# A hash-attention kernel with a feed-forward layer: another order for the first batch

## The chip, the cores and the metric

The kernel runs on one core of a Trainium2 chip. The metric is the device time of one execution in microseconds; lower is better. Profiles come from one profiled execution each, whose own time stands beside its span.

## What is computed

Four batches of eight heads attend over 768 positions with 64 values per head. Each query and key gets a bucket from six sign bits, and a query sees only the keys of its own bucket. The heads' outputs, side by side, are the input of a feed-forward layer that takes the largest of three products.

```python
q_bits = (np.einsum('bhsd,dk->bhsk', q, proj) > 0)      # 6 bits, k likewise
mask   = q_bucket[:, :, :, None] == k_bucket[:, :, None, :]
scores = np.where(mask, scale * q @ k.T, -1e9)
attn   = softmax(scores)                                 # + 1e-09 in the denominator
x      = (attn @ v) as [3072, 512]
h      = np.maximum(np.maximum(x @ w1, x @ w2), x @ w3)  # [3072, 768]
out    = h @ w_out                                       # [3072, 512]
```

## The kernel before

The mask is part of the matmul: six (or eight) rows of plus or minus one half stand below the 64 rows of queries and keys in the S tiles, so that a score of unequal buckets comes out far lower, and the exp takes it to almost nothing.

The work is cut into units. A unit is one head, half of the queries (384) and two of the six key blocks: `scores(u)` issues two matmuls into one of two PSUM buffers, and ScalarE takes the exp of both into a ring of 18 AT tiles. Six units make a group, which is one pair of heads and one half of the queries (`qh`); 32 groups make 192 units, 48 for each batch. The list `groups` sets their order.

When a group's six exps are done, `values(g)` (24 small matmuls) makes the attention output, and sums of the exps (24 small matmuls with ones) make the denominators. `far` does two groups with one set of sums: `part_values` twice, `part_sums`, `invert` (VectorE transposes and reciprocal, then five GpSimd copies that spread the result), and `scale` for each group, which writes `xT`. `near` does one group by itself without the GpSimd copies. The PSUM tile of the values has one buffer.

The feed-forward for half a batch (`ffn_groups(h)`) is 24 pieces: 18 of the first layer (four matmuls and a VectorE maximum each) and 6 halves of the second layer. It needs `xT` of all four pairs of that half. The list `ffn` hands out one piece per step.

The order is written out by hand and each engine runs its own instructions in that order (manual_schedule). Step u of the main loop issues `scores(u + 1)`, then what `when(u, ...)` put down for the step, then due steps such as `scale`, then one feed-forward piece if there is one, then what `firsts[u]` holds (values, sums), and from the second batch on a `burst` every twelve units.

Preparation of the first batch goes by pairs of heads. `pair_group` transposes three blocks on TensorE into PSUM and copies them to a T32 tile on VectorE; `pair_place` writes them as bfloat16 into S on GpSimd; `pair_hash` multiplies by the projection, VectorE makes the bits, and SyncE's queue sends them into S in four DMAs. Pair 0 has a way of its own (`first_hash`, `first_place`, `first_bits`), with its first unit started early. Later heads go by quads: `load_quad` and `load_v` load them, `turn` transposes on VectorE, `narrow` converts on GpSimd, `place` and `quad_hash` send into S by DMAs on SyncE's queue. `load_weights` loads w1, w2, w3 and w_out on GpSimd's queue.

Before, the first batch's groups are both halves of pair 0, both halves of pair 1, the first half of pairs 2 and 3, then their second half. So the first half of the queries is complete with the sixth group, and its feed-forward starts with step 40.

Of the kernel before, what the change touches and what calls it, by code (L numbers as in the profile page):

```python
# [9 lines left out]
FP32 = mybir.dt.float32  # L10
# [7 lines left out]
def kernel(  # L18
# [15 lines left out]
    P = 128  # L34
# [79 lines left out]
    def pair_keep(pi, side, hd, mp):  # L114
        if pi not in t32:
            t32[pi] = t32_pool.tile([P, 2, S], FP32, tag="T32", name="T32")
        nc.vector.tensor_copy(t32[pi][:, side, hd * HALF : (hd + 1) * HALF], mp[:, 0:HALF])  # L117

    def pair_place(pi, side, par, h0=0, h1=2):
        o = s_tile(pi)[0:D, 2 * side + h0 : 2 * side + h1, par * HALF : (par + 1) * HALF]  # L120
        i_ = t32[pi][par * D : (par + 1) * D, side, h0 * HALF : h1 * HALF].rearrange("d (h n) -> d h n", n=HALF)
        nc.gpsimd.tensor_scalar(out=o, in0=i_, scalar1=RS, scalar2=1.0, op0=AluOp.mult, op1=AluOp.mult)  # L122
# [27 lines left out]
    def first_hash(bp, side, hd):  # L150
        for par in range(2):
            j = 2 * side + par
            nc.tensor.matmul(bp[Q * j : Q * j + NBITS, 0:HALF], pj2[:, par : 2 * NBITS : 2],  # L153
                             t32[0][:, side, hd * HALF : (hd + 1) * HALF], start=True, stop=True)

    def first_bits(bp, side, hd, par):
        j = 2 * side + par
        nc.vector.tensor_scalar(out=s_of[0][D : D + NBITS, 2 * side + hd, par * HALF : (par + 1) * HALF],  # L158
                                in0=bp[Q * j : Q * j + NBITS, 0:HALF], scalar1=0.0, scalar2=0.5,
                                op0=AluOp.is_gt, op1=AluOp.subtract)  # L160
# [64 lines left out]


    groups = [(b, qh, jj) for b in range(B) for qh in range(2) for jj in range(HPAIR)]
    groups[0:8] = [(0, g % 2, g // 2) for g in range(4)] + [(0, g // 2, 2 + g % 2) for g in range(4)]
    NU = len(groups) * UPG
    UPB = NU // B  # L230
    xts, avs_of, av_of, sm_of = {}, {}, {}, {}
# [1 line left out]

    def unit_of(u):
        g, n = divmod(u, UPG)
        if g < 4:
            hd, n = divmod(u % (2 * UPG), UPG)
            return 2 * (g // 2) + n // MH, hd, n % MH
        return g, n // MH, n % MH

    def place_of(g, hd, kp):
        if g < 4:
            return (g // 2) * 2 * UPG + hd * UPG + (g % 2) * MH + kp
        return g * UPG + hd * MH + kp

    def scores(u):
        g, hd, kp = unit_of(u)
# [40 lines left out]
    def inverse(o, sm):  # L288
        ys = ys_pool.tile([P, HALF], FP32, tag="ys", name="ys")
        rr = small.tile([P, HALF // Q], FP32, tag="rr", name="rr")  # L290
        nc.vector.transpose(ys[:], sm[:, 0:HALF])
        nc.vector.tensor_scalar(out=rr[:], in0=ys[:, 0:HALF:Q], scalar1=EPS * S, scalar2=None, op0=AluOp.add)
        nc.vector.reciprocal(rr[:], rr[:])
        nc.vector.transpose(o, rr[:].unsqueeze(2).to_broadcast((P, HALF // Q, Q)))  # L294
# [25 lines left out]
    def far(gs):  # L320
        avs, sms, sb = [], [], []

        def part_values(i):
            if not sb:
                sb.append(small.tile([P, 2], FP32, tag="sv", name="sv"))
                sb.append(rb_pool.tile([P, 2, HALF], FP32, tag="rb", name="rb"))
            sv = sb[0]
            av = values(gs[i])
            avs.append(avs_pool.tile([P, HALF + 4], FP32, tag="avs", name="avs"))
            nc.vector.tensor_copy(avs[i][:, 0 : HALF + 1], av[:, 0 : HALF + 1])  # L330
            nc.gpsimd.tensor_scalar_mul(sv[:, i : i + 1], avs[i][:, HALF : HALF + 1], EPS)  # L331

        def part_sums():
            sms.append(ms_ps.tile([P, 512], FP32, tag="ms", name="sm"))
            for m in range(NM):
                for r in range(4):
                    nc.tensor.matmul(sms[0][Q * r : Q * (r + 1), 0:HALF], ones[:, :],  # L337
                                     at_of(gs[r % 2], m, r // 2)[:, 0:HALF], start=(m == 0), stop=(m == NM - 1))

        def invert():  # L340
            rb = sb[1]
            inverse(rb[:, 0, :], sms[0])
            nc.gpsimd.tensor_copy(rb[:, 1, :], rb[:, 0, :])  # L343
            for p0 in (0, D):
                nc.gpsimd.tensor_copy(rb[p0 + Q : p0 + D, 0, :], rb[p0 : p0 + Q, 0, :])  # L345
            for p0 in (0, D):
                nc.gpsimd.tensor_copy(rb[p0 : p0 + Q, 1, :], rb[p0 + Q : p0 + D, 1, :])  # L347

        def scale(i):
            sv, rb = sb  # L350
            nc.vector.scalar_tensor_tensor(out=xt_of(gs[i]), in0=avs[i][:, 0:HALF], scalar=sv[:, i : i + 1],  # L351
                                           in1=rb[:, i, :], op0=AluOp.add, op1=AluOp.mult)

        return part_values, part_sums, invert, [(6 + i, lambda i=i: scale(i)) for i in range(2)]


    def ffn_groups(h):
# [34 lines left out]
    def when(u, f, *args):  # L392
        at.setdefault(u, []).append(lambda: f(*args))

    with tc.manual_schedule():
# [39 lines left out]
            first_place(side, 0, par, mp)  # L435
            first_bits(bp, side, 0, par)
        pair_place(0, 0, 1, 0, 1)
        first_bits(bq, 0, 0, 1)
        mq1 = ms_ps.tile([P, 512], FP32, tag="ms", name="mp")
        pair_turn(0, 0, 1, mq1)  # L440
        scores(0)
        pair_keep(0, 1, 1, mk1)
        pair_keep(0, 0, 1, mq1)

        def first_rest():
            bps = [ms_ps.tile([P, 512], FP32, tag="ms", name="bp") for side in range(2)]
            for side in (1, 0):
                first_hash(bps[side], side, 1)
                for par in range(2):
                    pair_place(0, side, par, 1, 2)  # L450
            for side, par in ((1, 0), (0, 0), (1, 1), (0, 1)):
                first_bits(bps[side], side, 1, par)
            t32.pop(0)

        when(0, first_rest)

        for pi, us, uh in ((1, (1, 2, 3, 4), 6), (2, (8, 9, 14, 15), 16), (3, (17, 18, 19, 20), 21)):
            for u, (side, hd) in zip(us, ((1, 0), (1, 1), (0, 0), (0, 1))):
                when(u, pair_group, pi, side, hd)
                if hd == 1:  # L460
                    for par in range(2):
                        when(u, pair_place, pi, side, par)
            when(uh, pair_hash, pi)
        when(14, load_v, 1)
        for n, u in enumerate((1, 9, 22, 30)):
            when(u, load_weights, n)
        for u, side, g in ((8, 0, 2), (23, 1, 3), (25, 0, 3)):
            when(u, load_quad, side, g, range(4), nc.sync)
        hash_at = {}
        for g in range(2, NPAIR // 2):  # L470
            b2, i2 = divmod(g, 2)
            need = UPB * b2 + 12 * i2
            for n, side in enumerate((1, 0)):
                name = (side, g)
                if g > 3:
                    for x in range(4):
                        when(need - 36 + 4 * n + x, load_quad, side, g, (x,), nc.gpsimd)
                t0 = need - (24 if g == 2 else 21) + 4 * n
                for n2 in range(4):
                    when(t0 + n2, turn, name, n2 // 2, n2 % 2)  # L480
                for u2 in range(2):
                    when(t0 + 2 + 2 * u2, narrow, name, u2)
                when(t0 + 6, place, name, range(4))
            hash_at[{2: 34, 3: 50}.get(g, need - 12)] = g
            when({2: 33, 3: 44}.get(g, need - 22), load_v, g)

        ffn, steps = [], []
        ffn_at = {40: 0, 57: 1, **{24 * (h + 1) + 9: h for h in range(2, 2 * B - 1)}}

        def hash_due(u):  # L490
            if u in hash_at:
                when(u + 1, quad_hash(hash_at[u]))

        def burst(u, gs):
            vals, sums, invert, late = far(gs)
            vals(0)
            sums()
            hash_due(u)
            vals(1)
            invert()  # L500
            steps.extend((u + n, f) for n, f in late)


        firsts = {}

        def far_at(gs, us):
            vals, sums, invert, late = far(gs)
            for i, u in enumerate(us):
                firsts[u] = [lambda i=i: vals(i)]
            firsts[us[1] + 1] = [sums, invert, lambda: steps.extend((us[1] + 1 + n, f) for n, f in late)]  # L510

        def near_at(g, u):
            vals, sums = near(g)
            firsts[u], firsts[u + 1] = [vals], [sums]

        far_at((0, 1), (10, 12))
        far_at((2, 3), (22, 24))
        near_at(4, 30)
        near_at(5, 36)
        far_at((6, 7), (42, 48))  # L520
        for u in (34, 50):
            firsts[u] = [lambda u=u: hash_due(u)]

        for u in range(NU):
            if u + 1 < NU:
# [60 lines left out]
```

## Time and profile before

| | us |
|---|---|
| median of three runs | 288.41 |
| lowest and highest | 282.86, 288.48 |
| the profiled execution, its time | 283.91 |
| the profiled execution, its span | 282.1 |
| TensorE busy | 271.5 (96%) |
| VectorE busy | 177.1 (63%) |
| ScalarE busy | 166.5 (59%) |
| GpSimd busy | 106.6 (38%) |

In the profile PE is TensorE, PEld its weight loads, DVE is VectorE, ACT ScalarE, POOL GpSimd, SP SyncE; a q behind a name is the engine's queue of instructions. L255 is line 255 of the kernel. A row of the timeline gives start, duration, engine, line, operation, output and input, and in brackets how long the engine was idle before and what ended that. Matmul ends are modelled, so a busy TensorE is not always at its peak rate. The costliest lines are L257 (exp, 192 times, 153.5 us of ScalarE), L366 (first layer, 576 matmuls), L255 (scores, 384), L381 (second layer, 144), L281 (values, 768 small matmuls) and L337 (sums).

### The profile page before, as it was taken

The numbers are of one execution on the slowest core, as the hardware profiler recorded it, in microseconds if no ns is written. First come the engines' busy times: TensorE is split into PE (matmuls) and PEld (weight loads), VectorE is DVE, ScalarE is ACT, GpSimd is POOL, SyncE is SP. The second block draws the span as 40 slices with busy tenths as digits, with TensorE's granted clock in tenths as the row PEclk, the third lists the DMA queues.
The fourth block names the chain that finished last, engine by engine and source line by source line (L and its number), as shares of the span: only waits on it lengthen the run. The fifth ranks groups of instructions, "written<-read, shape, count | busy, mean of one in ns | idle before, by whom it ended". The sixth has DMA issues, their size and how long they took to land.

```text
span 282.1 us, 6387 instructions
## 1 busy us (share of the span) xinstructions
PE 271.5 (96%) x2476; PEld 145.7 (52%) x2476; DVE 177.1 (63%) x382; ACT 166.5 (59%) x220; POOL 106.6 (38%) x201
## 2 busy tenths in 40 slices
PE   8889989899999999999999999999999999999994
PEld 4444433454555554555555554555555555555551
DVE  3854785596635595796635594796536573568580
ACT  2586684763859485673858484764858485910102
POOL 3464957052209177452219096543021120303000
PEclk9999998999999999999999999999999999999999
DMA  7998689937115629682107439772020001100302
GB/s 223 322 186 183 107 156 220 243 53 137 42 39 171 130 37 217 163 187 72 30 37 197 103 58 217 195 138 71 1 77 37 2 0 41 74 2 2 112 0 112
DMA packets 21733, 30.99 MB, mean 110 GB/s; under 512 B 2616, under 2 KB 17096, under 8 KB 21704
## 3 DMA queue, kind: packets, MB, share of 16 engines
q0 software_dynamic: 8640, 12.59, 24.8%
q1 hardware_dynamic: 12776, 17.62, 21.8%
q8 instruction: 19, 0.31, 0.5%
q10 hardware_dynamic: 288, 0.39, 0.4%
q14 instruction: 10, 0.08, 0.1%
HBM read 25.17 MB, written 6.29 MB: 112 GB/s over the span
## 4 chain that ended last, share of the span: by engine, by line
PE 87%; DVE 7%; issue 2%; ACT 2%; DMA 1%; SPq 0%; DVEq 0%; ACTq 0%
PE l L366 30%; PE sc L255 20%; PE av L281 12%; PE l L381 11%; PE sm L337 5%; PE bp L197 3%; ACT AT L257 1%; PE wp L420 1%; DVE S L158 1%; DVE ht L372 1%; PE mp L111 1%; PE bp L133 1%; DMA S<-bits 1%; PE sm L308 1%; PE bp L153 1%
## 5 line engine op out<-in xcount | busy, mean ns | idle before, releaser
L257 ACT ACTIVATE AT<-sc 128x768 f16<-128x768 f32 x192 | 153.5, 813 | 79.5 <-PE sc L255 79.4
L366 PE MATMUL l<-xT,w_sb 128*128 128x384 f16 x576 | 113.2, 326 | 0.7 <-DVE ht L372 0.6
L255 PE MATMUL sc<-S 72*128 72x384 bf16 (+1 forms) x384 | 93.7, 328 | 4.0 <-ACT AT L257 2.1
L366 PEld LDWEIGHTS <-w_sb 128*128 128x128 f16 x576 | 55.9, 97 | 39.1 <-issue 1.2
L372 DVE TENSOR_TENSOR ht<-ht,l 128x384 f16<-128x384 f16 x96 | 52.5, 547 | 17.0 <-PE l L366 13.8
L255 PEld LDWEIGHTS <-S 72*128 72x128 bf16 (+1 forms) x384 | 35.0, 98 | 40.7 <-issue 17.0
L331 POOL TENSOR_SCALAR sv<-avs 128x1 f32<-128x1 f32 x30 | 6.4, 213 | 96.2 <-DVE avs L330 96.0
L330 DVE COPY avs<-av 128x385 f32<-128x385 f32 x30 | 16.8, 560 | 38.6 <-PE av L281 38.6
L281 PE MATMUL av<-AT,vo 128*32 128x385 f16 x768 | 38.2, 334 | 0.0
L381 PE MATMUL l<-wout_sb,ht 128*128 128x512 f16 x144 | 37.8, 379 | 0.4 <-DVE ht L372 0.4
L370 DVE CAST ht<-l 128x384 f16<-128x384 f32 x48 | 26.3, 547 | 15.9 <-PE l L366 15.2
L385 ACT COPY osb<-l 128x512 f32<-128x512 f32 x24 | 14.0, 582 | 27.9 <-PE l L381 27.9
L281 PEld LDWEIGHTS <-vo 128*32 128x32 f16 x768 | 18.9, 97 | 17.6 <-issue 9.6
L181 POOL TENSOR_SCALAR T<-T 128x768 bf16<-128x768 f32 x24 | 21.2, 885 | 15.0 <-DVE T L176 13.7
L176 DVE STREAM_TRANSPOSE T<-nat 128x384 f32<-128x384 f32 x48 | 26.2, 558 | 0.0
L381 PEld LDWEIGHTS <-ht 128*128 128x128 f16 x144 | 13.9, 97 | 14.5 <-DVE ht L372 1.8
L351 DVE SCALAR_TENSOR_TENSOR xT<-avs,sv,rb 128x384 f16<-128x384 f32 x30 | 19.7, 656 | 0.0
L337 PE MATMUL sm<-AT,ones 128*32 128x384 f16 x360 | 17.2, 326 | 0.0
L343 POOL COPY rb<-rb 128x384 f32<-128x384 f32 x15 | 7.5, 502 | 24.0 <-DVE rb L294 24.0
L122 POOL TENSOR_SCALAR S<-T 64x768 bf16<-64x768 f32 (+1 forms) x17 | 12.8, 754 | 7.5 <-DVE T L117 6.4
L347 POOL COPY rb<-rb 32x384 f32<-32x384 f32 x30 | 15.0, 500 | 1.5
L345 POOL COPY rb<-rb 32x384 f32<-32x384 f32 x30 | 15.0, 499 | 1.5
(43 smaller groups left out, 132.9 us busy)
## 6 DMA issues: line engine op xcount, KB each, us to landing
out_dram<-osb SPq DMA_DIRECT2D x24, 256.0 KB
S<-T SPq DMA_DIRECT2D x48, 96.0 KB
vo<-in_v_dram POOLq DMA_DIRECT2D x8, 384.0 KB, 6.5
nat<-in_k_dram POOLq DMA_DIRECT2D x16, 192.0 KB, 3.5
nat<-in_q_dram POOLq DMA_DIRECT2D x16, 192.0 KB, 6.0
w_sb<-in_moe_w_dram POOLq DMA_DIRECT2D x3, 768.0 KB, 9.1
nat<-in_k_dram SPq DMA_DIRECT2D x10, 192.0 KB
nat<-in_q_dram SPq DMA_DIRECT2D x8, 192.0 KB
```

What stands on the lines that cost most here:

```text
L176: nc.vector.transpose(t32[name][:, u, half * HALF : (half + 1) * HALF], i_)
L181: nc.gpsimd.tensor_scalar(out=t16[name][:, u, :], in0=t32[name][:, u, :], scalar1=RS, scalar2=1.0, op0=AluOp.mult, op1=AluOp.mult)
L255: nc.tensor.matmul(sc[:, j, 0:HALF], s_of[kn][0 : D + nb, kx, m * P : (m + 1) * P], s_of[qn][0 : D + nb, qx, qh * HALF : (qh + 1) * HALF], ...
L257: nc.scalar.activation(at_tiles[u % NAT][:, :, 0:HALF], sc[:, :, 0:HALF], ActFn.Exp, bias=-SCALE * 0.25 * nb, scale=SCALE)
L281: nc.tensor.matmul(av[hd * D + w * Q : hd * D + (w + 1) * Q, 0 : HALF + 1], vt[:, x, c * D + w * Q : c * D + (w + 1) * Q], at_of(g, m, hd) ...
L330: nc.vector.tensor_copy(avs[i][:, 0 : HALF + 1], av[:, 0 : HALF + 1])
L337: nc.tensor.matmul(sms[0][Q * r : Q * (r + 1), 0:HALF], ones[:, :], at_of(gs[r % 2], m, r // 2)[:, 0:HALF], start=(m == 0), stop=(m == NM ...
L351: nc.vector.scalar_tensor_tensor(out=xt_of(gs[i]), in0=avs[i][:, 0:HALF], scalar=sv[:, i : i + 1], in1=rb[:, i, :], op0=AluOp.add, op1=Alu ...
L366: nc.tensor.matmul(ps[:, 0:HALF], w_sb[wi][:, jc, fb * P : (fb + 1) * P], xt[:, jc, :], start=(jc == 0), stop=(jc == NJC - 1))
L370: nc.vector.tensor_copy(hts[fb][:], ps[:, 0:HALF])
L372: nc.vector.tensor_tensor(out=hts[fb][:], in0=hts[fb][:], in1=ps[:, 0:HALF], op=AluOp.max)
L381: nc.tensor.matmul(ps[:, 0:DM], hts[fb][:, tb * P : (tb + 1) * P], wout_sb[:, fb, :], start=(fb == 0), stop=(fb == NFB - 1))
```

## The change

The first batch's groups come in another order: pair 0 with both halves of the queries, then the first half of pairs 1, 2 and 3, then their second half. The first half of the queries is complete with the fifth group. The feed-forward starts with step 34. Pairs 2 and 3, the quads of the second batch and the weights are prepared in other steps, `far` and `near` take other groups, the spreading of the denominators on GpSimd is a step of its own (`spread`), and the preparation of pair 0's second head is spread over two steps.

```diff
-    groups[0:8] = [(0, g % 2, g // 2) for g in range(4)] + [(0, g // 2, 2 + g % 2) for g in range(4)]
+    groups[0:8] = [(0, 0, 0), (0, 1, 0)] + [(0, qh, jj) for qh in range(2) for jj in range(1, HPAIR)]
...
         def invert():
+            inverse(sb[1][:, 0, :], sms[0])
+
+        def spread():
             rb = sb[1]
-            inverse(rb[:, 0, :], sms[0])
             nc.gpsimd.tensor_copy(rb[:, 1, :], rb[:, 0, :])
...
         pair_place(0, 0, 1, 0, 1)
-        first_bits(bq, 0, 0, 1)
         mq1 = ms_ps.tile([P, 512], FP32, tag="ms", name="mp")
         pair_turn(0, 0, 1, mq1)
         scores(0)
         pair_keep(0, 1, 1, mk1)
         pair_keep(0, 0, 1, mq1)
...
+        first_bits(bq, 0, 0, 1)
...
-        when(0, first_rest)
+        when(0, first_rest, 1)
+        when(1, first_rest, 0)
 
-        for pi, us, uh in ((1, (1, 2, 3, 4), 6), (2, (8, 9, 14, 15), 16), (3, (17, 18, 19, 20), 21)):
+        for pi, us, uh in ((1, (1, 2, 3, 4), 6), (2, (5, 7, 8, 9), 11), (3, (14, 15, 16, 17), 18)):
...
-        when(14, load_v, 1)
-        for n, u in enumerate((1, 9, 22, 30)):
+        when(10, load_v, 1)
+        for n, u in enumerate((1, 14, 20, 26)):
             when(u, load_weights, n)
-        for u, side, g in ((8, 0, 2), (23, 1, 3), (25, 0, 3)):
+        for u, side, g in ((12, 0, 2), (20, 1, 3), (22, 0, 3)):
...
-                t0 = need - (24 if g == 2 else 21) + 4 * n
+                t0 = need - (28 if g == 2 else 21) + 4 * n
...
-            hash_at[{2: 34, 3: 50}.get(g, need - 12)] = g
+            hash_at[{2: 29, 3: 50}.get(g, need - 12)] = g
...
-        ffn_at = {40: 0, 57: 1, **{24 * (h + 1) + 9: h for h in range(2, 2 * B - 1)}}
+        ffn_at = {34: 0, 57: 1, **{24 * (h + 1) + 9: h for h in range(2, 2 * B - 1)}}
...
-        far_at((0, 1), (10, 12))
-        far_at((2, 3), (22, 24))
+        far_at((0, 1), (10, 12, 13), (19, 22, 23))
+        far_at((2, 3), (19, 24, 25), (25, 30, 31))
         near_at(4, 30)
-        near_at(5, 36)
-        far_at((6, 7), (42, 48))
-        for u in (34, 50):
+        far_at((5, 6), (36, 42, 43), (43, 49, 50))
+        near_at(7, 48)
+        for u in (29, 50):
```

In the new `far_at` the steps are, in order: values of the first group, values of the second, sums and inverse; then the spread, and the scaling of the first and of the second group.

More of the change, by code (lines that the diff above doesn't have):

```diff
@@ L235, in unit_of @@
         g, n = divmod(u, UPG)
[L236 to L238 removed]
+        if g < 2:
+            hd, n = divmod(u, UPG)
+            return n // MH, hd, n % MH
         return g, n // MH, n % MH
     def place_of(g, hd, kp):
[L242 to L244 removed]
+        return hd * UPG + g * MH + kp if g < 2 else g * UPG + hd * MH + kp
     def scores(u):
@@ L352, in scale @@
                                            in1=rb[:, i, :], op0=AluOp.add, op1=AluOp.mult)
-        return part_values, part_sums, invert, [(6 + i, lambda i=i: scale(i)) for i in range(2)]
+        return part_values, part_sums, invert, spread, [lambda i=i: scale(i) for i in range(2)]
     def ffn_groups(h):
@@ L443, with first_rest @@
         pair_keep(0, 0, 1, mq1)
[L445 to L453, printed above, removed]
-        when(0, first_rest)
-        for pi, us, uh in ((1, (1, 2, 3, 4), 6), (2, (8, 9, 14, 15), 16), (3, (17, 18, 19, 20), 21)):
+        first_bits(bq, 0, 0, 1)
+        bps = {}
+        def first_rest(side):
+            bps[side] = ms_ps.tile([P, 512], FP32, tag="ms", name="bp")
+            first_hash(bps[side], side, 1)
+            for par in range(2):
+                pair_place(0, side, par, 1, 2)
+            if side == 0:
+                for sd, par in ((1, 0), (0, 0), (1, 1), (0, 1)):
+                    first_bits(bps[sd], sd, 1, par)
+                t32.pop(0)
+        when(0, first_rest, 1)
+        when(1, first_rest, 0)
+        for pi, us, uh in ((1, (1, 2, 3, 4), 6), (2, (5, 7, 8, 9), 11), (3, (14, 15, 16, 17), 18)):
             for u, (side, hd) in zip(us, ((1, 0), (1, 1), (0, 0), (0, 1))):
@@ L494, in burst @@
         def burst(u, gs):
-            vals, sums, invert, late = far(gs)
+            vals, sums, invert, spread, late = far(gs)
             vals(0)
@@ L500, in burst, with far_at @@
             invert()
-            steps.extend((u + n, f) for n, f in late)
+            spread()
+            steps.extend((u + 6 + n, f) for n, f in enumerate(late))
         firsts = {}
[L506 to L510, printed above, removed]
+        def far_at(gs, us, us2):
+            vals, sums, invert, spread, late = far(gs)
+            for u, fs in zip(us + us2, ([lambda: vals(0)], [lambda: vals(1)], [sums, invert], [spread], late[0:1], late[1:])):
+                firsts.setdefault(u, []).extend(fs)
         def near_at(g, u):
             vals, sums = near(g)
-            firsts[u], firsts[u + 1] = [vals], [sums]
-        far_at((0, 1), (10, 12))
-        far_at((2, 3), (22, 24))
+            firsts.setdefault(u, []).append(vals)
+            firsts.setdefault(u + 1, []).append(sums)
+        far_at((0, 1), (10, 12, 13), (19, 22, 23))
+        far_at((2, 3), (19, 24, 25), (25, 30, 31))
         near_at(4, 30)
-        near_at(5, 36)
-        far_at((6, 7), (42, 48))
-        for u in (34, 50):
-            firsts[u] = [lambda u=u: hash_due(u)]
+        far_at((5, 6), (36, 42, 43), (43, 49, 50))
+        near_at(7, 48)
+        for u in (29, 50):
+            firsts.setdefault(u, []).append(lambda u=u: hash_due(u))
         for u in range(NU):
```

## The prediction

> **What bounds the kernel now.** I read the page's shares first, then the clock row, then the timeline of TensorE through the first batch, then the chain.
>
> ```profile
> PE 271.5 (96%) x2476; PEld 145.7 (52%) x2476; DVE 177.1 (63%) x382; ACT 166.5 (59%) x220; POOL 106.6 (38%) x201
> PEclk9999998999999999999999999999999999999999
> PE 87%; DVE 7%; issue 2%; ACT 2%; DMA 1%; SPq 0%; DVEq 0%; ACTq 0%
> ```
>
> TensorE is busy 96% and carries 87% of the chain. An order that keeps its work can gain only where it waits. From the step with the first feed-forward group on, exps start every 0.98 us, which is 0.65 us of feed-forward and 0.33 us of a score pair: no wait. So what can be won lies before that.
>
> ```profile
> 20.95 0.81 PE L255 MATMUL sc<-S 70*128 70x384 bf16 x4 [0.52 <-DMA S<-bits]
> 33.58 1.17 PE L281 MATMUL av<-AT,vo 128*32 128x385 f16 x24
> 36.96 1.16 PE L337 MATMUL sm<-AT,ones 128*32 128x384 f16 x24
> 39.51 0.48 PE L255 MATMUL sc<-S 70*128 70x384 bf16 x2 [0.63 <-ACT AT L257]
> 41.63 2.12 PE L281 MATMUL av<-AT,vo 128*32 128x385 f16 x24
> 46.99 0.48 PE L255 MATMUL sc<-S 70*128 70x384 bf16 x2 [0.63 <-ACT AT L257]
> 53.67 0.48 PE L255 MATMUL sc<-S 70*128 70x384 bf16 x2 [0.63 <-ACT AT L257]
> 53.99 1.08 PE L366 MATMUL l<-xT,w_sb 128*128 128x384 f16 x4
> ```
>
> The columns are start, length, engine, line, operation, and the idle time before with what ended it. Step u issues scores(u+1), then its other work. The first row is step 11 (unit 12 waited for pair 1's hash bits), the seventh is step 40, the last the first feed-forward group. Those 32.72 us (53.67 - 20.95) hold 29 steps. TensorE's work in them: 29 score pairs x 0.326 (L255) = 9.45; 5 values x 1.10 = 5.50; 4 sums x 1.09 = 4.36; 6 transpose trios (L111) x 0.49 = 2.94; 2 pair hashes x 0.85 = 1.70; the quad hash 1.43 (values, sums and quad hash from the chain). Sum 25.38, so 7.34 us are waits. They are: score pairs that wait for the exp two units earlier, because only two score buffers exist (the three rows with 0.63 and their followers, about 3.0); two hashes held by the copies of their transposes (26.12 to 27.82, and 31.15 to 33.14: 0.85 + 1.15); a stretch at half clock (1.65, below); some 0.7 unassigned. ScalarE's own pace is 0.74 per exp in a run (five take 3.70), so a step with nothing but scores lasts 0.74 and leaves TensorE 0.41 idle.
>
> ```profile
> 38.00:40.00 2.00, 1.36 (x10) 0.50 (x6) 1.73 (x5) 1.35 (x2) 0.10 (x1) 1.00 1.13 201
> 40.00:42.00 2.00, 1.53 (x12) 0.53 (x16) 2.00 (x5) 1.91 (x4) 1.84 (x4) 0.76 1.13 244
> 42.00:44.00 2.00, 2.00 (x26) 0.70 (x18) 1.10 (x3) 0.61 (x1) 1.79 (x4) 0.50 1.11 255
> 44.00:46.00 2.00, 2.00 (x29) 0.86 (x28) 0.35 (x1) 0.81 (x1) 1.86 (x3) 0.88 1.13 221
> ```
>
> These are stretches of 2 us: busy time of TensorE, its weight loads, VectorE, ScalarE and GpSimd, then the granted clock, DMA share and GB/s. After the thin 38 to 41 us the clock is 0.5 to about 44.5. Its price: the values at 41.63 took 2.12 for 1.17 (0.95), two score pairs before them 1.28 for 0.82 (about 0.4), one after them 0.82 for 0.50 (0.3). Together 1.65 us.
>
> **The change, part by part.** TensorE's instructions stay the same in number and kind, so I compare one stretch in both orders.
>
> *Start.* The second-half query bits of head 0 go behind two copies on VectorE, and their PSUM buffer comes free later. In the new order scores(1) waits for exp(0) (end 9.22 + 0.81 = 10.03) where it waited for bits until 9.86, and scores(2) waits for those bits: copies from 9.3, bits until about 10.9, scores at 11.1 where they were at 11.67 behind both hashes. The 0.2 us of scores(1) is made good there; bounds 0.3 either way, taken as 0.
>
> *Two more trios (steps 5, 7) ahead of unit 12*, 0.98 us: half of them fits into the 0.52 us wait for the bits. The trio of step 5 also puts one copy (0.56) ahead of pair 1's bits on VectorE. Scores(12) come 0.4 later, at 21.35.
>
> *The stretch.* Units 12 to 40 in the new order: scores 9.45; 5 values 5.50 (steps 12, 19, 24, 30, 36); 3 sums 3.27 (13, 25, 31; one moves from 37 to 43); 4 trios 1.96; 2 hashes 1.70; quad hash 1.43 (step 29 for 34); and six feed-forward groups (34 to 39) x 0.65 = 3.90. Sum 27.21. Waits: a step that carries under 0.41 us besides its scores lasts 0.74. Up to step 19 every step but 10 carries a trio, a hash, values or sums, so none waits on ScalarE for long. Steps 20 to 23 and 26 to 28 carry nothing else, and 32 and 33 neither. The first two of such a run issue from the backlog, each later one waits 0.41 and the first to wait 0.74: 0.74 + 0.41 + 0.41 (22 to 24), 0.74 + 0.41 (28, 29), 0.74 (34) = 3.45. From 34 on the feed-forward fills them.
>
> *The moved preparations.* Pair 3's hash moves to step 18 with its first use at step 23. Bits end to scores took 3.46 us for pair 1 (17.49 to 20.95); with the hash's end near 29.7 and 0.6 for VectorE, units 24 on can start at 33.75, against 33.35 by TensorE: 0.4 of wait. Pair 2: bits end 23.2, usable 26.7, wanted 27.8: none. On GpSimd's queue pair 3's four placements (0.8 each) end near 30.8, the delayed spread (2.6) near 33.4, w3's issue near 34.4; w3 then takes 9.1 (the page's median), so 43.5 against its first use near 47. On SyncE's queue the quad loads stand behind pair 2's and pair 3's bits (four x 0.82 each), landing near 31 and 38 to 41, wanted at 35 and in step 39. VectorE is the tight one: eight transposes x 0.56, two copies, an inverse (1.6) and two scalings between 31 and 40. The quad hash at step 29 needs the last transpose, which I put at 39.9 against 40.1 when TensorE reaches that half: 0, or 0.6 if VectorE slips one instruction.
>
> *First feed-forward group.* Sums at step 31, scaling 2.5 us after their end (as 45.60 to 48.16), group at step 34: the same 0.3 wait that makes the 1.08 above out of 0.81.
>
> *Half clock.* Before shows one stretch; I keep one, 1.65, bounds 0 and 4.95 (three). The row speaks for it: 2.29 us of work in the 3.4 us ahead of the dip sufficed, and steps 20 to 23 carry 4 x 0.33 = 1.3 in 2.95. The Trainium skill (TensorE: Matmul & The Clock Gate, Part 1) has the half clock come after an idle window of about 3.4 us, in windows that run freely. By that rule neither order has a stretch that qualifies, and the sum would be without the 1.65, which is rival A's time; the trace disagrees, since it shows the dip without such an idle window.
>
> *Steady part and end.* The groups run six steps earlier from then on, so which steps hold GpSimd and VectorE work shifts; before loses 0.4 at three places (exps 1.46 apart instead of 0.98), and I expect as many, bounds -1.2 and +0.8. Behind the last unit 34 groups stand instead of 40: four of the first layer, then six halves of the second, while VectorE inverts. The final values end at 251.4, the spread behind them at 256.44, two scalings of 0.61 later it is 257.7: 6.3 us, which the ten groups (6.7) still cover; the second layer's first tile waits 0.4 for its input.
>
> *Sum.* 27.21 + 3.45 + 0.4 (pair 3) + 0.3 (first group) + 0.7 (unassigned, as before) + 1.65 = 33.7, from 21.35: step 40 begins at 55.05, 1.4 later than before, with 3.90 of feed-forward done and 1.09 of sums still due. Gain 3.90 - 1.09 - 1.38 = 1.4, less 0.4 at the end: 1.0. Against the profiled execution, 283.91 (span 282.1), that is 282.9. The runs shown have a median of 288.41 and reach from 282.86; my sum stands at their lower end.
>
> **The rivals.** A: no half clock. Feed-forward six steps earlier covers the place where the dip was. Time 282.9 - 1.65 = 281.2. Against it: steps 20 to 23 are thinner than what went ahead of the dip.
>
> B: slower, through half clock. Steps 20 to 23 and 26 to 28 are both thin, and the values and sums of 24, 25, 30 and 31 follow at once. Each stretch costs 1.65. With two the time is 284.55, already above 283.91, with three 286.2. For it: 44% of work (1.3 in 2.95) against 67% (2.29 in 3.4). Against: the first 38 us before hold steps as thin for a short while, without a dip.
>
> C: the runs of before differ by 5.6 us, more than three such stretches; if the early waits make that spread, filling them brings every run down: about 281.5 where before's median is 288.41, 2.4% less. Against: one execution was profiled, and no view shows the others.
>
> D: pair 3's bits land late. Weights, quads and bits share the DMA between 24 and 35 us, where before has shares of 0.8 to 1.1. If the landing takes the 6.5 us that the page has for a load of v, then scores(24) wait 3 us more: 285.9.
>
> E: the groups move and their gain is eaten by the thin steps: 283.9, no change.
>
> **How the numbers follow.** Forecast (282.9) 0.34, A 0.20, B 0.15, C 0.18, D 0.06, E 0.07. About 2% (5.7 us) is what a measurement tells here. Faster by over 2%: C and a third of A, 0.25. Slower by over 2%: B and D at once (286.2 + 3.0 = 289.2) with the other late landings, 0.09. Within: 0.66. Range: low 279.0, A with the 1.2 of the steady part and without the waits for bits and at the end; high 288.0, B with three stretches (286.2) and VectorE's 0.6 and 1.2 of D. The likeliest's own range is 281.5 to 284.5.
>
> **What would show it.** The first feed-forward matmul at about 47.5 us (45.9 without half clock) instead of 53.99; pairs of scores with waits for exps in steps 22 to 24 and 28; a 0.4 us wait for bits near 33.5; a clock below 1 once between 33 and 45. Wrong if the clock dips twice or more, if w3 or the bits hold TensorE, or if the steady part loses a step's time at every burst.

## The result, and the profile after

| | before | after |
|---|---|---|
| median of six runs, us | 282.96 | 286.05 |
| lowest and highest, us | 282.25, 288.48 | 284.32, 287.35 |
| the profiled execution, us | 283.91 | 286.07 |
| its span, us | 282.1 | 284.3 |
| its mean granted clock | 0.994 | 0.987 |

The ratio after to before is 1.011, with the interval 1.0073 to 1.0147: the change made the kernel about 3 us slower, less than the 2% but more than its uncertainty. The forecast was 282.9, with a gain of 1.0. The comparison leaves disturbed runs out, which is why the ratio does not use every run of the table.

The page of after, the rows that answer to those of before:

```profile
PE 269.1 (95%) x2476; PEld 144.8 (51%) x2476; DVE 177.9 (63%) x382; ACT 166.2 (58%) x220; POOL 107.2 (38%) x201
PEclk9999959999999999999999999999999999999999
PE 80%; DMA 8%; DVE 4%; POOL 3%; issue 1%; SPq 1%; ACT 1%; POOLq 0%; ACTq 0%; DVEq 0%
```

The instructions are the same in number. TensorE's share of the chain fell from 87% to 80%, and DMA rose from 1% to 8%. The clock's row has a 5 in the sixth slice (a slice is 7.1 us) where before has an 8 in the seventh. So a transfer sets the pace somewhere, and a longer half clock begins earlier. The timeline of TensorE in after says where:

```profile
21.31 0.49 PE L253 MATMUL sc<-S 70*128 70x384 bf16 x2 [1.17 <-DMA S<-bits]
33.08 0.48 PE L253 MATMUL sc<-S 70*128 70x384 bf16 x2 [0.63 <-ACT AT L255]
36.92 1.44 PE L253 MATMUL sc<-S 70*128 70x384 bf16 x4 [3.36 <-DMA S<-bits]
38.29 2.12 PE L279 MATMUL av<-AT,vo 128*32 128x385 f16 x24
41.10 1.35 PE L335 MATMUL sm<-AT,ones 128*32 128x384 f16 x24
51.22 0.65 PE L366 MATMUL l<-xT,w_sb 128*128 128x384 f16 x3
52.19 0.32 PE L366 MATMUL l<-xT,w_sb 128*128 128x384 f16 x1 [0.32 <-DVE xT L312]
58.45 0.49 PE L253 MATMUL sc<-S 70*128 70x384 bf16 x2
192.75 0.48 PE L253 MATMUL sc<-S 72*128 72x384 bf16 x2 [0.95 <-DMA S<-T]
```

The first row is scores(12), at the predicted time (21.35). The third is scores(24), the first unit of pair 3: it waited 3.36 us for pair 3's hash bits where 0.4 was predicted. The first feed-forward group starts at 51.22, and step 40's scores at 58.45 instead of 55.05. The last row is a second wait that before does not have, for a transposed tile in the fourth batch's preparation.

The chain through the first wait, in after:

```profile
30.20 0.57 DVE bits L137
30.78 0.74 SPq L142
31.57 5.22 DMA S<-bits
36.92 1.44 PE sc L253 x4
```

The bits were made at 30.77, early enough (the prediction had 30.3). The transfer then took 5.22 us, where pair 1's took 2.96 in the same execution. SyncE's queue tells what stood ahead of it:

```profile
17.20 9.11 SPq L142 DMA_DIRECT2D S<-bits  x8
26.35 2.21 SPq L170 DMA_DIRECT2D nat<-in_q_dram  x4
30.78 3.05 SPq L142 DMA_DIRECT2D S<-bits  x4
33.94 2.57 SPq L170 DMA_DIRECT2D nat<-in_k_dram  x4
```

Rows of L142 send bits, rows of L170 load quads. Quad (0,2), 768 KB of queries, was issued from 26.35 to 28.56, after pair 2's bits and ahead of pair 3's. VectorE waited for its last block until 36.38. And this is what the DMA did from 28 to 30 us (packets, MB, share of 16 engines by queue):

```profile
DMA packets 273, 0.42 MB, mean 210 GB/s; under 512 B 0, under 2 KB 273, under 8 KB 273
q0 software_dynamic: 273, 0.42, 115.4%
```

All of it went to GpSimd's software queue, where w2's load had been issued at 25.07; SyncE's hardware queue, with the quad waiting in it, does not appear. From 32 to 34 us the hardware queue moved 0.48 MB, which is the quad, and only then came the bits. So pair 3's 36 KB stood behind a quad, and the quad behind w2. The Trainium skill (DMA: Bandwidth & Descriptors, Queues, rings and completion order) says that a queue row keeps one ring per DMA engine and that an engine goes round the rows packet by packet. The order within SyncE's queue agrees with that; in the two microseconds without a packet of the hardware queue no turns were taken, or the quad's packets were not ready; the trace does not tell which.

The granted clock in after, in stretches of 2 us (columns as in the prediction):

```profile
34.00:36.00 2.00, 0.00 (x0) 0.00 (x0) 1.54 (x3) 0.47 (x1) 1.81 (x4) 0.68 0.46 99
36.00:38.00 2.00, 1.07 (x4) 0.43 (x4) 0.58 (x1) 0.18 (x1) 1.84 (x3) 0.50 1.03 238
38.00:40.00 2.00, 2.00 (x26) 0.77 (x24) 0.00 (x0) 1.33 (x2) 0.30 (x1) 0.50 0.97 182
40.00:42.00 2.00, 2.00 (x30) 0.67 (x26) 1.04 (x2) 0.73 (x1) 0.22 (x1) 0.61 1.11 227
```

TensorE does nothing from 34 to 36 us, and the half clock runs from 34.7 to 41.5: 6.8 us where before has 3.4 (41.05 to 44.46).

**Where the time went.** Step 40 begins 4.78 us later than before (58.45 against 53.67), with 2.81 more of work done (six feed-forward groups, 3.90, less the sums still due, 1.09). That is a loss of 1.97. The wait at 192.75 loses 1.1 (two exps start 2.09 apart instead of 0.98), and the steady part wins back 0.9 to 1.0: in before, exps start 1.46 and 1.45 apart instead of 0.98 at 108.08 and 170.70, and in after they do not. The end loses nothing: from the end of the last unit's values it is 26.8 us in after and 30.7 in before, which is the six groups of 0.65. Together 2.1 to 2.2, against 2.2 between the spans.

### The profile page after: what moved, and what is told of

Same layout as the page of the kernel before. It is cut to its first block, busy times and chain, and to the rows that moved or that the text cites. A ratio compares the mean times of both kernels' runs of the same rounds, so it can differ in the third digit from the quotient of the medians.

```text
span 284.3 us, 6384 instructions
## 1 busy us (share of the span) xinstructions
PE 269.1 (95%) x2476; PEld 144.8 (51%) x2476; DVE 177.9 (63%) x382; ACT 166.2 (58%) x220; POOL 107.2 (38%) x201
## 4 chain that ended last, share of the span: by engine, by line
PE 80%; DMA 8%; DVE 4%; POOL 3%; issue 1%; SPq 1%; ACT 1%; POOLq 0%; ACTq 0%; DVEq 0%
PE l L366 29%; PE sc L253 20%; PE av L279 11%; PE l L381 10%; PE sm L335 5%; DMA S<-T 4%; DMA S<-bits 3%; PE bp L197 2%; PE mp L111 1%; DMA pst<-in_proj_dram 1%; POOL nat L170 1%; PE bp L153 1%; PE bp L133 1%; PE sm L306 1%; POOL T L181 1%
## 5 line engine op out<-in xcount | busy, mean ns | idle before, releaser
L181 POOL TENSOR_SCALAR T<-T 128x768 bf16<-128x768 f32 x24 | 20.4, 850 | 10.3 <-DVE T L176 8.9
L347 POOL COPY rb<-rb 32x384 f32<-32x384 f32 x30 | 16.3, 543 | 1.5
L345 POOL COPY rb<-rb 32x384 f32<-32x384 f32 x30 | 15.0, 499 | 1.5
```

Source lines behind the costliest of these rows:

```text
L181: nc.gpsimd.tensor_scalar(out=t16[name][:, u, :], in0=t32[name][:, u, :], scalar1=RS, scalar2=1.0, op0=AluOp.mult, op1=AluOp.mult)
```

## The experiments

Each of the twelve ran beside the kernel before on the same chip, and its ratio is to those runs. Their median was 283.95 us for the first four experiments below, 283.54 for the next four and 284.18 for the last four, so ratios compare better than medians. Waits are TensorE's, taken from one profiled execution each.

**Quad (0,2) ahead of both pairs' bits.** The changed kernel with:

```diff
-        for u, side, g in ((12, 0, 2), (20, 1, 3), (22, 0, 3)):
+        for u, side, g in ((8, 0, 2), (20, 1, 3), (22, 0, 3)):
```

> The changed kernel with one thing put back: the query quad (0,2) is loaded in step 8, as before the change, not in step 12. Theory Q (order in SyncE's queue): pair 3's bits were issued at 30.78 us behind that quad's four loads, which moved nothing between 26 and 30 us while w2 was being loaded, so the bits landed 5.2 us after their issue. With the quad ahead of pair 2's bits the 3.36 us wait before scores(24) falls to under 0.8 us, TensorE is not idle there, the half-clock stretch is one window or none, and the time falls by 3 to 4 us, to 282 to 283. Theory T (thin steps 20 to 23 by themselves, and pair 3's preparation too late whatever the queue holds): the wait stays above 2.5 us and the time at 285 to 286.

Measured: median 285.05, ratio 1.0053 (1.0011 to 1.0096), profile 283.86. Timeline of TensorE, the row of scores(24):

```profile
34.68 1.03 PE L253 MATMUL sc<-S 70*128 70x384 bf16 x4 [0.42 <-ACT AT L255]
```

The wait for bits is gone, and only the exp holds scores(24). w2's load was where it had been (25.77 to 33.28; 25.07 to 33.32 in after). One half-clock stretch is left (35.65 to 39.07). From scores(12) to step 40 it took 33.89 us (22.00 to 55.89), against 33.3 by the prediction's sum without its 0.4 for bits. So the sum of that stretch was sound but for the transfer. The time missed the expected 282 to 283 and is the one that theory T gave, though not for its reason: the wait near 192 us stayed (1.3), and the kernel was still slower than before.

**w2 and w3 later, the quad where the change put it.**

```diff
-        for n, u in enumerate((1, 14, 20, 26)):
+        for n, u in enumerate((1, 19, 23, 26)):
             when(u, load_weights, n)
```

> The changed kernel with the load of w2 in step 19 (not 14) and of w3 in step 23 (not 20); the quad's place in the queue stays. Theory Q with its second half (the quad crawls because w2's 1.6 MB are on the DMA engines from 25 us): the quad lands by 30 us, the bits land under 3 us after their issue, the wait before scores(24) is under 1 us, time 282.5 to 284 unless w3 comes late for the third feed-forward group, which would show as a wait of that group. If the quad crawls by itself, or the bits are late for another reason, the wait stays near 3.4 us.

Measured: median 283.88, ratio 0.9994 (0.9946 to 1.0041), profile 282.45 without any half clock. Timeline of TensorE:

```profile
33.70 1.02 PE L253 MATMUL sc<-S 70*128 70x384 bf16 x4 [0.42 <-ACT AT L255]
50.17 0.82 PE L366 MATMUL l<-xT,w_sb 128*128 128x384 f16 x4 [0.88 <-DMA w_sb<-in_moe_w_dram]
```

The order on SyncE's queue is that of after, and yet scores(24) found their bits: without w2 on the DMA the quad had moved by the time the bits were issued at 30.50. Smaller waits for bits remain (0.27 at scores(12), 0.23 at scores(18), 0.74 at scores(27), which need pair 3's other bits, and 0.84 at 126.92, 2.1 in all). So the queue's order alone is not the cause. The price is w3, which now arrives 0.88 us late. The wait near 192 us does not occur here.

**Pair 3's bits on ScalarE's queue.**

```diff
-                nc.sync.dma_start(s_of[pi]...
+                eng = nc.scalar if pi == 3 else nc.sync
+                eng.dma_start(s_of[pi]...
```

> The changed kernel with pair 3's four bits loads issued on ScalarE's queue instead of SyncE's. Theory Q: on another queue they don't stand behind the quad, and land 1 to 2.5 us after their issue; the wait before scores(24) falls to 0 to 1.5 us, while ScalarE pays about four times 0.5 us of issuing; time 283 to 285. Rival S (the DMA engines themselves are full between 30 and 36 us, whatever the order): they land 4 us or more after their issue, and the wait stays above 2.5 us.

Measured: 288.98, two runs, ratio 1.0139 (1.0001 to 1.0277), where 283 to 285 was expected. ScalarE's queue was held for 4.57 us by the four issues (31.22 to 35.79), the exps stood behind them, and TensorE waited 4.20 for an exp. The run moved the wait. The bits were not quick on that queue either: from 33 to 36 us it moved 0.02 MB, beside 0.59 MB on SyncE's. Whether the slow issues or the full DMA (rival S) held them, the run does not tell.

**Feed-forward from step 40 again, with the new order.**

```diff
-        ffn_at = {34: 0, 57: 1, ...
+        ffn_at = {40: 0, 57: 1, ...
```

> The changed kernel with the feed-forward from step 40, as before the change. Six groups of 0.65 us move from steps 34 to 39 to the end, and those steps go back to the pace of ScalarE. By the sums of the prediction the steps 34 to 39 then hold 0.74 + 0.41 + 0.74 us of waits again: 1.9 us more than the changed kernel, about 288. If the early groups bring nothing because something else (w3, VectorE, the order at the end) takes it back: no difference within 0.5 us.

Measured: median 288.6 of four runs, ratio 1.011 (1.002 to 1.0201). The medians differ by 2.5 from after's, but the ratios are equal, and runs with the same granted clock differ by 0.9 to 2.1. What the early feed-forward is worth is not settled by this run. The wait near 192 us does not occur in it.

**Quad early and thin steps filled.** Here `fill` is two matmuls of warm-up data whose product nobody reads, 0.33 us.

```diff
+        for u in (20, 21, 22, 23, 26, 27, 28, 32, 33):
+            when(u, fill)
```

On top of quad (0,2) in step 8:

> The kernel with the quad in step 8 again, plus two matmuls whose result nobody reads (0.33 us) in each thin step: 20 to 23, 26 to 28, 32 and 33. They fit under the pace of ScalarE, so they cost about 0. Theory H (what is left of the loss, and the spread of the runs, is the half clock after thin stretches): the granted clock is 0.998 or more in nearly all runs, they lie within 1.5 us of each other, and the median falls from 285.05 to 282.3 to 283.3. If the half clock has nothing to do with how thin those steps are, clock, spread and median stay as they were without the filling (0.98 to 1.0, 5.6 us, 285).

Measured: median 285.62, ratio 1.0112 (1.0065 to 1.0159). The wait moved to pair 2, whose bits now stood behind the quad (their transfer took 5.63 us; with the same order and without the fill, scores(18) had not waited):

```profile
30.20 0.80 PE L253 MATMUL sc<-S 70*128 70x384 bf16 x2 [2.06 <-DMA S<-bits]
```

The half clock followed it, from 29.9 to 36.7, so this profile tells nothing about thin steps. But two of the four runs had a granted clock of 0.999 and 1.0 and still took 285.11 and 284.59, more than any run of before at 1.0 beside them (281.98 to 283.54): what was left of the loss is not half clock alone, as theory H had it.

**The kernel before with its thin steps filled** (steps 23, 26 to 29, 32, 33, 38 and 39):

> The kernel before the change with the same two idle matmuls in its thin steps 23, 26 to 29, 32, 33, 38 and 39. Theory H: its runs had clocks from 0.98 to 1.0 with times from 282.28 to 289.39, so filled they lie at 282.3 to 283.5, against a median of 283.95 unfilled. Otherwise the spread stays, or the filling costs its 9 x 0.33 = 3 us. How it stands to the filled new order tells what the order itself is worth without half clock: by the prediction's sums the new one is 1 to 2 us faster, less the about 1 us that the trace shows lost near 190 us.

Measured: median 285.07, ratio 1.0022 (0.9974 to 1.007), ten runs from 282.37 to 287.81, their mean clocks from 0.986 to 1.0. Filling neither slowed the kernel nor removed the half clock or the spread.

**Weights late and quad early, filled.**

```diff
-        for n, u in enumerate((1, 14, 20, 26)):
+        for n, u in enumerate((12, 16, 20, 26)):
```

> As the filled kernel with the quad in step 8, but w1 is loaded in step 12 instead of 1 and w2 in step 16 instead of 14. Pair 1's bits then don't share the DMA with w1: the wait before scores(12), 1.45 us with w1 in step 1, falls to under 0.5 us and the time by about 1 us, to 281.5 to 282.5. Rival: the weights come late for the first feed-forward groups at step 34 to 36, or pair 3's bits wait for w1 and w2; then one wait is exchanged for another and the time is the same or longer.

Measured: 286.69, ratio 1.0154 (1.0099 to 1.0209), not 281.5 to 282.5. The wait before scores(12) went, as expected, and the rival came true: waits for bits of 2.21 at scores(18) and 3.07 at scores(24). The second is the one that matters for the cause. Timeline of TensorE, chain, and what the DMA did from 30.1 to 35.2 us:

```profile
38.36 0.48 PE L253 MATMUL sc<-S 70*128 70x384 bf16 x2 [3.07 <-DMA S<-bits]
```

```profile
32.95 5.27 DMA S<-bits
```

```profile
q0 software_dynamic: 589, 0.88, 105.2%
```

SyncE's queue had moved 0.78 MB, the quad, between 22 and 27 us, so nothing stood ahead of pair 3's bits. They were issued from 32.18 on, and in those 5 us SyncE's queue moved nothing: the row shown is the software queue with w1 and w2. So the load of weights held the bits by itself, as long as the quad and w2 together did in after (5.22). Moving the bulk loads by a few steps only chose which pair's bits met them.

**The later quads loaded three steps earlier.** On top of quad (0,2) in step 8 and the fill:

```diff
-                        when(need - 36 + 4 * n + x, load_quad, side, g, (x,), nc.gpsimd)
+                        when(need - 39 + 4 * n + x, load_quad, side, g, (x,), nc.gpsimd)
```

> As the filled kernel with the quad in step 8, but the quads of the third batch and later are loaded three steps earlier. It is about the wait of 0.95 to 1.3 us near 190 us, which the changed kernel has and the one before has not: if it is late loading (GpSimd's queue of loads ahead of the narrowing, then placing, then the bits), it goes away and the time falls by about 1 us against the filled kernel. If it is the six steps' shift of the output stores in SyncE's queue, which stand ahead of the placing, it stays.

Measured: median 282.59, ratio 0.9978 (0.9936 to 1.0021). The wait near 192 us is gone. Against the run without this edit the ratio fell from 1.0112 to 0.9978; part of that is the wait at pair 2's bits, 1.17 us in this profile and 2.06 in the other, and only one of the two profiles has a half clock.

**Only the later quads earlier, on the changed kernel.**

> The changed kernel, with one edit: the quads of the third batch on are loaded three steps earlier. Theory (two separate losses, pair 3's bits behind the quad near 34 us and a wait for a transposed tile near 192 us): the first stays at 3 to 4 us of wait at scores(24), the second (0.95 us at the matmul, 1.1 us between the exponentials) goes; 1.0 to 1.3 us less than the changed kernel, so about 285.0, still at or above the kernel before. Rival (the second wait is only a shift that moves elsewhere): within 0.3 us of the changed kernel's 286.05.

Measured: median 285.37, ratio 1.0039 (0.9992 to 1.0086). Step 40 begins at 58.33, as in after (58.45), and scores(24) wait 3.66 for bits; the span is 283.0, 1.3 less. The wait near 192 us is gone, so that loss and the wait for bits are two separate ones. This profile has one half-clock stretch (37.74 to 41.16) where after has two.

**Quad (0,2) behind pair 3's bits**, in step 19, its transposes three steps later, the hash of quad 2 in step 32, and the later quads earlier:

```diff
-        for u, side, g in ((12, 0, 2), (20, 1, 3), (22, 0, 3)):
+        for u, side, g in ((19, 0, 2), (20, 1, 3), (22, 0, 3)):
...
-            hash_at[{2: 29, 3: 50}.get(g, need - 12)] = g
+            hash_at[{2: 32, 3: 50}.get(g, need - 12)] = g
```

> The changed kernel, with quad (0,2) loaded in step 19, behind pair 3's bits, instead of step 12, its transposes in steps 27 to 30 and the hash of batch 2 in step 32, and the later quads three steps earlier. Theory (order on SyncE's queue sets pair 3's bits): no wait for bits at scores(18) over 1.2 us and at scores(24) under 0.8 us; step 40 within 1.0 us of 55.1; 281.0 to 283.0 us, 3 to 5 us less than the changed kernel and about 1 less than the kernel before where the clock stays full. Rival (the software queue's load of w2 alone starves the bits, whatever stands ahead of them on SyncE's queue): the wait at scores(24) stays over 2 us and the time is 284.5 to 286. Second rival (the quad now comes too late, and its hash or its transposes hold DVE): the wait moves to steps 32 to 48 with 1 to 3 us, 284 to 285.

Measured: median 281.24 of four runs (279.66 to 284.58), ratio 0.9875 (0.9798 to 0.9951). Its profile is the slowest of the four, with two half-clock stretches and a wait of 2.19 at scores(12), where this order does nothing new; so its step 40 begins at 58.06 and not near 55.1. Pair 2's and pair 3's bits held nobody, and no new wait appeared in steps 32 to 48 (the second rival). The first rival (w2 alone starves the bits) was hardly put to the test: w2 kept its step, but in this late execution it landed at 35.31, while the bits were issued from 34.38 to 37.40.

**The same, filled** (steps 20 to 23, 26 to 28 and 33):

> As the run with quad (0,2) in step 19, and two more matmuls of 0.33 us, whose product nobody reads, in each of steps 20 to 23, 26 to 28 and 33. Theory (the half clock follows waits of 2 us and more, not thin steps): with no such wait left, no half clock before 45 us in either kernel and the same time within 0.7 us. Rival (thin steps bring the half clock): this one shows none and the run without the fill shows one window of 3.4 us, and this one is 1.5 to 3 us faster.

Measured: median 280.47 of four runs (279.73 to 282.54), ratio 0.9878 (0.9804 to 0.9952). Timeline of TensorE and, below, SyncE's queue:

```profile
22.52 0.48 PE L253 MATMUL sc<-S 70*128 70x384 bf16 x2 [2.45 <-DMA S<-bits]
36.78 0.48 PE L253 MATMUL sc<-S 70*128 70x384 bf16 x2
49.26 0.81 PE L366 MATMUL l<-xT,w_sb 128*128 128x384 f16 x4
56.01 0.49 PE L253 MATMUL sc<-S 70*128 70x384 bf16 x2
```

```profile
17.13 19.46 SPq L142 DMA_DIRECT2D S<-bits  x12
36.64 1.86 SPq L170 DMA_DIRECT2D nat<-in_q_dram  x4
```

All twelve sends of bits now stand ahead of quad (0,2), and scores(24) at 36.78 wait for nothing. Here too w2 had landed (33.58) when pair 3's bits were issued (33.57 on). From scores(12) to step 40 it took 33.49 us, where the prediction's sum had 33.7 with one half-clock stretch; this execution has one too (from 24.4, right after the wait at scores(12)). Theory expected no half clock before 45 us: wrong, as each had one after the wait at scores(12). The unfilled run had a second from 44.5, without a wait of 2 us ahead of it, and the filled one did not, as the rival had it; but the ratios are the same, so the 1.5 to 3 us that the rival put on the fill were not there. These two are the fastest versions, about 1.2% faster than before.

**w2 and w3 later, and the later quads earlier.**

> The changed kernel, with w2 loaded in step 19 and w3 in step 23, and the later quads three steps earlier. Theory (w2's load on the software queue held up the quad, and the quad the bits): waits for bits under 0.5 us at scores(18) and scores(24) as in the run with w2 late alone, w3 late by about 1 us near 50 us, no wait near 192: 1.0 to 1.3 us less than the 283.88 of w2 late alone, so about 282.7, and 0.5 to 1.3 less than the kernel before. Rival (the late w2 and w3 cost what the bits gain): 283.5 to 284.5, no different from the kernel before.

Measured: median 282.19 of ten runs (281.26 to 283.12), ratio 0.9947 (0.9913 to 0.998). Faster than before by 0.5%, as expected from w2 late (0.9994) and the wait near 192 us removed. In its profile scores(18) and scores(24) wait for no bits and w3 is in time, but scores(27) wait 0.98 for pair 3's other bits: their last send took 5.36 us beside w2, with the quad already moved.

## Why the prediction was wrong, point by point

**The moved preparations: the step that failed.** The term "0.4 (pair 3)" was mis-sized: scores(24) waited 3.36 us for pair 3's bits (3.66 in the run with the later quads earlier). The prediction priced the bits with 3.46 us from their end to their use, which is pair 1's row, with w1's load beside it but no quad issued just ahead; in after it was 6.15 (30.77 to 36.92). By the steps of the new order (pair 2's hash 11, quad (0,2) 12, pair 3's hash 18) that quad goes ahead of pair 3's bits, and w2's load runs beside both. The prediction's sentence on that queue puts the quads behind pair 2's and pair 3's bits and asks when they land ("near 31" for the first; VectorE had to wait until 36.38 for its last block), not what a quad does to the bits behind it. That the bits hold TensorE was among its own signs of being wrong.

Two edits each took the wait away with the other condition left in place: the quad loaded earlier with w2's load where it was, and w2 later with the queue's order unchanged (scores(24) wait 0.42 in both, for an exp). So in the changed kernel the wait came from the two together: w2 kept the quad back until 30 us, and the quad's packets then went ahead of the bits. It does not always take both: where the weights were loaded in steps 12 and 16, their load alone made the bits take 5.27 us. In the profiles of the two kernels with the quad behind the bits, w2 was about done when the bits were issued, so they do not show what the bits would cost beside it.

Rival D had the right wait at scores(24), the right size (3 us) and the right time (285.9 against 286.05), with a chance of 0.06. Its reason, that weights, quads and bits share the DMA there, is the right one as far as it goes; it did not look at what stands ahead in the queue.

**Half clock.** One stretch at 1.65 was forecast. After has two back to back. Their price is 2.1: 0.95 at the values (2.12 for 1.17), 0.62 at scores(24) and their followers (1.44 for 0.82), 0.32 at one score pair and 0.19 at the sums. It is less than rival B's two times 1.65, because 2.2 us of the first stretch fell into the wait. B put it down to thin steps; here TensorE stood still for 3.36 us. The wait alone does not set their number: without it the profiles have one stretch (quad in step 8), none (w2 late) and two (quad in step 19), and with it the run with only the later quads earlier has one.

**Steady part.** Forecast unchanged. It lost 1.1 at 192.75, where the chain runs back through a transfer of a transposed tile (S<-T, 8.65 us) to seven quad loads and a load of v that GpSimd issued between 170.6 and 177.3, its conversions between them. And it won 0.9, as before's losses did not occur. The prediction read three of 0.4; the trace has two, where exps start 1.46 and 1.45 apart. Net 0.2, within the bounds given, but by two terms that the prediction did not see. The wait near 192 us is in none of the five kernels that load three steps earlier, and in five of the seven that keep the changed kernel's loading steps (not with w2 late, nor with the feed-forward from step 40).

**Right.** The waits for exps: 0.63 at 33.08, and again after 42 us. The first group's wait for its scaled input, 0.32 (0.3). Pair 2's bits held nobody. w3 was in time, though it landed at 47.67 and not at 43.5, because step 40 came late too. The sum of the stretch, 33.3 without its 0.4 for bits, holds to about 0.6 us where pair 3's bits are in time: 33.89 with the quad in step 8 and 33.49 with it in step 19 and the fill, each with one half-clock stretch. With w2 late, without half clock, it took 34.09, of which 1.85 are waits for bits and w3 that the sum does not have, against 31.65.

**Luck.** Scores(12) at 21.31 (21.35 forecast) is right in part by luck: the first exp began at 8.22 where before has 9.22, the wait for pair 1's bits was 1.17 where before has 0.52, and the same order put scores(12) anywhere from 20.88 to 23.33 in other kernels.

**The end.** The forecast took 0.4 off the gain there. Nothing was lost: TensorE waits 0.62 in both kernels, and the second layer's first tile does not wait.

**Sum.** 282.9 + 2.96 (3.36 for 0.4, bits) + 0.45 (half clock) + 1.1 - 0.9 (steady part) - 0.4 (end) = 286.1; the profiled execution took 286.07.

**Rival A and the gain.** At a granted clock of 1.0, the kernels whose scores(24) found their bits take 279.66 to 282.92 us, on both sides of rival A's 281.2 (without the filled one whose pair 2 waited 2.06; it took 284.59); before takes 281.98 to 283.54. With the quad in step 8 the profile has one half clock like before's and before's span (282.1), although it loses 1.5 near 190 us. So the new order does gain in the early part, and the bits took it back. How much of the 1.2% of the fastest versions is the order's was not measured: it is 3.4 us where 1.0 was forecast, and the kernel before was not run with its later quads loaded earlier.

**Rival C.** That the spread of before's runs comes from its early waits: filling its thin steps left the spread (282.37 to 287.81), so thin steps alone do not make it. What starts a half clock in before stays open.

## What to carry to other kernels

When preparation steps are moved, write each DMA queue's new order down, transfer by transfer, and beside it what the other queues carry at that time: here 36 KB that the next matmul needed came late behind a 768 KB load of data for later, and late again behind nothing but a load of weights on another queue. Price a small transfer from a row in which the same things stand ahead of it and run beside it. And when a reordering loses time, first look whether one of its parts put a bulk load ahead of an urgent one. Between the two kernels that both load the later quads early, moving quad (0,2) by seven steps, with its transposes and hash, took the kernel from 0.4% slower than before (0.9992 to 1.0086) to 1.2% faster.

## What the runs showed of the hardware that was not expected

**The run time goes with the half-clock stretches.** Each stretch in these profiles lasts a multiple of 3.41 us, and a mean clock of 0.994 over 282 us is one of them (0.5 x 3.41 / 282 = 0.006). In one group of runs of before, at a clock of 0.997 or more, times lie between 282.4 and 283.1; at 0.994 between 283.4 and 286.5, all but one at or under 284.2; at 0.982 between 288.2 and 289.3. Three stretches at the 1.65 us worked out above would be 5.0 of the 5.7 or so between 0.982 and the full clock, which is most of the spread that the three runs shown at first had; the rest may be the waits that go with them, which only a profile would show. In none of after's six runs did the clock reach 1.0 (0.982 to 0.994).

**A half clock does not need an idle window.** Eleven of the fourteen profiles (before, after and twelve experiments) show a stretch in the first 64 us. Ahead of each, TensorE was busy for 2.29 us or less of the preceding 3.4, and four times 2.29 or 2.30: steps of 0.74 us that wait for exps. But thin spans of the same depth passed without one (1.81 of 3.4 with w2 late, ending at 40.65). The Trainium skill (TensorE: Matmul & The Clock Gate, Part 1) describes windows of 3.4 us that run freely, whatever the kernel does; the lengths agree with it, and so do the starts: the two stretches with the quad in step 19 begin at 24.00 and 44.48, six times 3.41 apart. A free phase would help to explain why the same order of work dips in one run and not in the next, but phase and busy time are not all: with only the later quads earlier, the 3.41 us from 30.92, two windows ahead of that run's stretch, held 2.13 of work, less than the 2.29 that sufficed elsewhere, and no half clock followed at once. That the window must be idle does not agree. The threshold was not measured.

**A wait's size in one execution is not its size.** Up to scores(12), eight of these kernels issue the same work. Scores(12) began at 20.88 in one and 23.33 in another, with waits just before them from 0.1 to 2.9 us. Pair 1's bits took 2.96 us in after and 4.70 with the feed-forward from step 40, both beside w1's load; why was not found.
